# Eight early products of a folded weight placed between second products of a channel MLP, and one PSUM bank emptied by VectorE instead of ScalarE

## The chip, the cores and the metric

The kernel runs on one core of one Trainium2 chip. The metric is device time in microseconds of one execution, taken as the median of several executions. The engines are named as in the profile: PE is TensorE (matmul), PEld its weight load, DVE is VectorE, ACT is ScalarE, POOL is GpSimd, and SP is SyncE, which here only issues DMA.

## The reference, cut to what matters

```python
x = A_x                                   # (1, 2048, 640), float32
xn = layernorm(x)
return x + A(xn, wqkv, w_phi, wo) + B(xn, w1, b1, w2, b2)

# A: linear attention, 32 heads of 20
q, k, v = split_heads(xn @ wqkv)
pq, pk = q @ w_phi[h], k @ w_phi[h]       # per head
phi = lambda p: concat(softmax(p), softmax(-p))
o = phi(pq) @ (phi(pk).T @ v) / (phi(pq) @ phi(pk).sum(0) + 1e-6)
A = merge_heads(o) @ wo

# B: channel MLP with 1728 hidden units
B = gelu(layernorm(xn) @ w1 + b1) @ w2 + b2
```

All of it is float32. The kernel carries each float32 operand as two parts, a high one and a low one (`split`: ACT rounds the high part, DVE or POOL subtracts it to get the low part), and multiplies in three passes: high by high, high by low, low by high (`mm3`, L69 to L72).

## The kernel before, in words

The 2048 tokens are four blocks of 512 (b = 0 to 3), the 640 channels five chunks of 128 (KC = 5), the 1728 hidden units fourteen chunks of 128, taken in pairs (g = 0 to 6, j = 0 and 1).

**Order of the whole.** PE's order is written out by hand for the whole kernel (`manual_schedule` for PE, L513). From L562 to L865 the orders of DVE, ACT and POOL are written out too: each of them does its instructions in the order of the program text. From L865 to L1350 a list scheduler orders DVE, ACT and POOL by the program's order and by what it reckons to be ready, and after that they are by hand again. SP's queue of DMAs is put in order by the list scheduler throughout: a DMA whose buffer is free and whose data is there can be issued long before its place in the text. `tc.issue_after(loads[1])` keeps a DMA behind the load `loads[1]` in SP's queue, and nothing else.

**The channel MLP.** `passes(g, b, ws)` (L286) first does the pair's two first products (`first`, L275): for each j five chunks of three matmuls into one of the banks 0 to 2, then `gelu` (L282): ACT reads the bank, applies GELU with the bias into the tile `gt`, copies the high part to `hh`, and DVE subtracts for `hl`. After the first `yield` come the second products: for each output chunk m = 0 to 4, six matmuls (two j, three passes) into one of the banks 5 to 7 in turn, and a DVE instruction that adds the bank to `acc[b]` (L326 for g = 0, L328 otherwise). Three banks in turn mean that chunk m can only begin when the bank used three chunks earlier has been added up.

**Work beside it.** `tick()` is called after each three matmuls of a first product and after each j of a second one. It takes one step of the generator `mlp.beside`, and this is how other work is laced into the engines' orders.

**The start.** `p00` is the pair g = 0 on block 0, whose first products come from `half_first`; `p10` is the pair g = 1 on block 0. The order on PE is: `half_first`, the first products of `p10` (10 ticks), the second products of `p00` (10 ticks), the second products of `p10` (10 ticks), then `p01` and `p11` (block 1). The generator beside is `next_y` (L610), which makes the operand of block 1: at its fourth tick it sends the rows of mean and inverse deviation to DRAM on ACT's queue (L202) and loads them back, spread over 128 partitions, on SP's queue (`load_rows`, L207; this DMA is `loads[1]`). Later, once every two ticks, POOL subtracts the mean from a chunk of `acc[1]` (L635), DVE multiplies (L637), ACT copies the high part (L639), DVE subtracts (L641).

**The fold.** `wpt` is w_phi (120 rows, 6 groups of 6 by 20) with its first column subtracted from the 19 others (L662, one DVE instruction). The fold multiplies it into wk and wq: fourteen lists of up to four units (`units`), taken in seven jobs of two lists (`jobs`). For a job `raws` loads two tiles of transposed wk or wq (L683), `products` (L692) does four products of each tile into one of the banks 3 and 4 (`mlp.px`), and `split_w` (L700) moves each bank into the tiles `wk` by ACT (L711) and DVE (L713). The generator `prep` (L738) runs this beside `p11` and later passes; its first job's products are its first step. Tiles of the fold are in the pool `prep`, which is opened after the pool of the starting loads has been closed. In the same pool are `t` (rows of x for further statistics, L730) and `xq` (four tiles for chunks of blocks 2 and 3, loaded at L764, 10 loads in all, used far later).

**The start of the second part.** After the projections, whose exponentials are ACT's L934 (on POOL's L933), block 2 begins: L1094 makes `passes(0, 2, ws)`, and its two first products and the last key tile (`kv_tile`, L965) follow each other on PE, then the first products of block 3 (L1331). They share the banks 0 to 2 (`ptile`): j = 0 of block 2 has a first bank, j = 1 a second, the last key tile the third, and j = 0 of block 3 needs the first again. `issue_after(exps["q", 15].ins)` at L1095 keeps ACT's instructions of block 2 behind the last exponential on ACT.

Of the kernel before, what the change touches and what calls it, by code (L numbers as in the profile page):

```python
# [8 lines left out]
F32 = mybir.dt.float32  # L9
F32R = mybir.dt.float32r  # L10
AF = mybir.ActivationFunctionType
ALU = mybir.AluOpType
# [34 lines left out]
def f(ap):  # L47
    return ap.bitcast(F32)
# [3 lines left out]
def tile_kernel(ctx: ExitStack, tc: tile.TileContext, x, xT, wkT, wqT, wv, wphi, wo, w1, b1, w2, b2,  # L52
                ident, mmask, emask, vsel, out):
    nc = tc.nc
    ctx.enter_context(nc.allow_low_precision(reason="float32 operands are split exactly into float32r parts"))

    def split(hi, lo, src, scale=None, eng=nc.vector, first=nc.scalar):

        if scale is None:
            if first is nc.scalar:  # L60
                nc.scalar.activation(hi, src, AF.Copy)  # L61
            else:
                first.tensor_copy(hi, src)
            eng.tensor_tensor(lo, src, f(hi), op=ALU.subtract)  # L64
        else:
            nc.scalar.activation(hi, src, AF.Copy, scale=scale)
            nc.vector.scalar_tensor_tensor(lo, src, scale, f(hi), op0=ALU.mult, op1=ALU.subtract)

    def mm3(ps, lh, ll, rh, rl, first, last, **kw):  # L69
        nc.tensor.matmul(ps, lh, rh, start=first, stop=False, **kw)  # L70
        nc.tensor.matmul(ps, lh, rl, start=False, stop=False, **kw)  # L71
        nc.tensor.matmul(ps, ll, rh, start=False, stop=last, **kw)  # L72
# [47 lines left out]
    def mtile(i, dtype=F32):  # L120
        return mp.tile([P, 2, D if i < 5 else 512], dtype, name=f"m{i}")
# [82 lines left out]
    def load_rows(b, i=5):  # L204

        mr = mtile(i)
        loads[b] = nc.sync.dma_start(mr.rearrange("p a t -> p (a t)"),  # L207
                          (r_dram[1][0] if b == 1 else r_dram[2][b - 2]).rearrange("r t -> (r t)").unsqueeze(0).to_broadcast([P, 8 * P])).ins
        return mr

    loads = {}


    class Mlp:
# [60 lines left out]
        def first(self, g, j, b, w, gt, hh, hl):  # L275
            pz = self.ph()
            for kc in range(KC):
                mm3(pz, w[0][:, kc, :], w[1][:, kc, :], y[b][0][:, kc, :], y[b][1][:, kc, :], kc == 0, kc == KC - 1)
                self.tick()
            self.gelu(g, j, pz, gt, hh, hl)  # L280

        def gelu(self, g, j, pz, gt, hh, hl):  # L282
            nc.scalar.activation(gt, pz, AF.Gelu_apprx_tanh, bias=b1t[:, 2 * g + j:2 * g + j + 1])  # L283
            split(hh, hl, gt)

# [280 lines left out]
    def step(gen, n):  # L566
        for _ in range(n):
            next(gen, None)
# [38 lines left out]
    p00 = mlp.passes(0, 0, [wc[0], wc[1]], hid)  # L607
    next(p00)

    def next_y():  # L610
# [12 lines left out]
        for _ in range(8):  # L623
            yield

        for c in range(2, 4):
            parts[c][1]()
        for _ in range(5):
            yield
        xcs = {}  # L630
        for n in range(2 * KC + 5):
            c, i = divmod(n, 2)
            if i == 0 and c < KC:
                xcs[c] = xp.tile([P, D], F32, name="xb")[:, :512]
                nc.gpsimd.tensor_tensor(xcs[c], acc[1][:, c], mr[:, 0], op=ALU.subtract)  # L635
            if i == 0 and 0 <= (d := c - 1) < KC:
                nc.vector.tensor_tensor(xcs[d], xcs[d], mr[:, 1], op=ALU.mult)  # L637
# [12 lines left out]
    xs.close()  # L650
    with tc.issue_after(loads[1]):
# [2 lines left out]
    wkv = ExitStack()  # L654
    kvw = wkv.enter_context(tc.tile_pool(name="wkv", bufs=1, side="right", reuse_waits="tile"))
    wkv_ = [kvw.tile([P, KC, CN], F32R, name=f"wk{p}") for p in "hl"]
    rs = ExitStack()
    fp = rs.enter_context(tc.tile_pool(name="prep", bufs=2, side="right", reuse_waits="tile"))
    wpt = fp.tile([G6, 6, 6, DH], F32, name="wpt", bufs=1)
    with tc.issue_after(loads[1]):  # L660
        nc.sync.dma_start(wpt, wphi)
    nc.vector.tensor_tensor(wpt[:, :, :, 1:], wpt[:, :, :, 1:], wpt[:, :, :, 0:1].to_broadcast([G6, 6, 6, DF]), op=ALU.subtract)  # L662

    units = [(n, g, i) for n in "kq" for g in range(5) for i in range(KC)]
    units = [units[o:o + 4] for o in range(0, 50, 4)] + [[("kq", 5, i) for i in range(KC)]]

    def by_group(us):

        gs = [u[:2] for u in us]
        return [(*g, gs.index(g), gs.count(g), slice(us[gs.index(g)][2], us[gs.index(g)][2] + gs.count(g)))
                for g in dict.fromkeys(gs)]

    def raws(batch):
        ts = []
        for us in batch:
            raw = fp.tile([P, D], F32, name="raw")
            for n, g, u, nu, i in by_group(us):
                r, kk = g * G6, G6 if g < 5 else 2 * DH  # L680
                for j, one in enumerate(n):
                    with tc.issue_after(loads[1]):
                        nc.sync.dma_start(raw[j * kk:(j + 1) * kk, u * P:(u + nu) * P],  # L683
                                          {"k": wkT, "q": wqT}[one][r:r + kk, i.start * P:i.stop * P])
            ts.append(raw)
        return ts

    def prep_fold(batch, ts):

        parts = {"k": [(0, 0, DF)], "q": [(KQ, 0, B1F), (C3, B1F, DF)]}  # L690

        def products(us, raw):  # L692
            ps = mlp.px()
            for u, (n, g, i) in enumerate(us):
                nh = 6 if g < 5 else 4
                nc.tensor.matmul(ps[:, u * nh * DF:(u + 1) * nh * DF], raw[:nh * DH, u * P:(u + 1) * P], wpt[:nh * DH, g, :nh, 1:],  # L696
                                 start=True, stop=True)
            return us, ps
# [37 lines left out]
        yield from rows(2, 2, fp, mlp.px, 5)  # L736

    def prep():  # L738
        jobs = [units[o:o + 2] for o in range(0, 14, 2)]
# [14 lines left out]
        raw = fp.tile([P, D], F32, name="raw").rearrange("p (c d) -> p c d", c=KC)  # L754
# [5 lines left out]
        xs, hls, events = {}, {}, []  # L760

        def load(c, b):
            xs[c, b] = fp.tile([P, 512], F32, name="xq", bufs=4)
            nc.sync.dma_start(xs[c, b], xT[c * P:(c + 1) * P, b * 512:(b + 1) * 512])  # L764

        def centred(c, b):
            nc.gpsimd.tensor_tensor(xs[c, b], xs[c, b], mr[b][:, 0], op=ALU.subtract)
# [241 lines left out]
    for t, i in [(t, i) for t in range(14) for i in range(4)] + TAIL:  # L1009
        if (t, i) in ((4, 0), (8, 0)):  # L1010
            b = t // 4 + 1
# [3 lines left out]
        ps = proj(t, i)  # L1015
# [29 lines left out]
        if (t, i) == (11, 0):  # L1045
            mlp = Mlp((0, 3, 2, 1), ((1, 2), (0, 3)))
# [434 lines left out]
```

## Time and profile before

| what | value |
|---|---|
| median of 3 runs | 716.25 us (715.61 to 716.4) |
| the profiled execution | 716.96 us |
| its span, first to last instruction | 715.2 us |
| mean granted TensorE clock | 0.999 |
| busy: PE, DVE, POOL, ACT | 704.0, 513.1, 421.7, 342.1 us |
| fold products on PE (L696, 110 instructions) | 13.3 us |

A row of a timeline is: start in us from the first instruction, length in us, engine, line, operation, out<-in, shape, count, and in brackets the time for which the engine had been idle and what ended that. A row of the waits is: who waited for what, then total us, times, longest us. A row of the chain of waits is: start, us, what was on the chain. The engine names SPq and ACTq mean the queue of instructions that issue DMAs. A product of two plain float32 operands is two instructions on PE, so the eight products of a job are 16.

### The profile page before, as it was taken

To read this page: it belongs to the slowest core of one execution; us is meant where nothing else is said; L and a number is where in the kernel's file an instruction comes from. 1 tells how busy PE (TensorE), PEld (TensorE's weight loads), DVE (VectorE), ACT (ScalarE), POOL (GpSimd) and SP (SyncE) were. 2 spreads that over 40 slices of the span, in tenths; PEclk is the share of its full clock that TensorE was granted. 3 is DMA by queue.
4 is the path that set the end of the run, shared out by engine and by line. 5 is a ranking of instruction groups with operands and counts; after the bars stand their busy time and mean duration, and the time that the engine had idled before them with its cause. 6 is when DMAs were issued, how large, how long until landed. Compare 5 with 4: busy or idle time off the path is not lost.

```text
span 715.2 us, 9745 instructions
## 1 busy us (share of the span) xinstructions
PE 704.0 (98%) x3381; PEld 591.2 (83%) x3381; DVE 513.1 (72%) x820; ACT 342.1 (48%) x563; POOL 421.7 (59%) x360
## 2 busy tenths in 40 slices
PE   8989999999999999999999999999999999999998
PEld 6868888878878888888888888888888878888886
DVE  7776754978754788788888877747679785784632
ACT  6434453444433544554444547357666666560200
POOL 3521223657235998798787979548689887540400
PEclk9999999999999999999999999999999999999999
DMA  9813643474722226325500708864355568545222
GB/s 325 290 44 110 196 134 102 154 243 159 224 91 110 74 91 219 97 89 196 121 0 13 177 0 322 223 205 125 109 160 168 171 181 274 188 127 212 80 83 73
DMA packets 65767, 106.56 MB, mean 149 GB/s; under 512 B 7462, under 2 KB 31814, under 8 KB 63838
## 3 DMA queue, kind: packets, MB, share of 16 engines
q1 hardware_dynamic: 65414, 105.93, 46.5%
q8 instruction: 26, 0.43, 0.2%
q14 instruction: 23, 0.19, 0.1%
q10 hardware_dynamic: 304, 0.01, 0.0%
HBM read 71.37 MB, written 34.55 MB: 148 GB/s over the span
## 4 chain that ended last, share of the span: by engine, by line
PE 79%; DVE 7%; POOL 4%; DMA 4%; issue 3%; ACT 2%; SPq 1%; POOLq 0%; DVEq 0%; ACTq 0%
PE bank L898 23%; PE bank L70 16%; PE bank L72 15%; PE bank L71 15%; PE bank L968 2%; PE bank L696 2%; POOL m L933 2%; PE bank L1206 1%; PE bank L1207 1%; POOL w L64 1%; DMA t<-t 1%; DMA xq<-in_xT 1%; POOL m L944 1%; PE bank L323 1%; PE bank L324 1%
## 5 line engine op out<-in xcount | busy, mean ns | idle before, releaser
L898 PE MATMUL bank<-wkh,y 128*128 128x512 f32 (+1 forms) x480 | 139.5, 364 | 0.0
L70 PE MATMUL bank<-y,w 128*128 128x512 f32 (+1 forms) x294 | 114.4, 389 | 1.0 <-ACT m L283 1.0
L71 PE MATMUL bank<-y,w 128*128 128x512 f32 (+1 forms) x294 | 113.6, 387 | 0.0
L72 PE MATMUL bank<-y,w 128*128 128x512 f32 (+1 forms) x294 | 113.6, 386 | 0.0
L64 POOL TENSOR_TENSOR w<-r,w 128x640 fp32r<-128x640 f32 x32 | 52.2, 1645 | 98.8 <-ACT w L61 68.0
L70 PE MATMUL bank<-m,w 128*128 128x512 f32 x260 | 102.7, 395 | 3.5 <-DVE acc L328 3.2
L72 PE MATMUL bank<-m,w 128*128 128x512 f32 x260 | 101.3, 390 | 0.0
L71 PE MATMUL bank<-m,w 128*128 128x512 f32 x260 | 101.3, 389 | 0.0
L898 PEld LDWEIGHTS bank<-wkh,y 128*128 128x128 f32 x480 | 87.5, 188 | 13.3
L898 PE MATMUL bank<-wkl,y 128*128 128x512 f32 (+1 forms) x240 | 87.4, 364 | 0.0
L70 PEld LDWEIGHTS bank<-y,w 128*128 128x128 f32 x294 | 55.2, 188 | 12.8 <-ACT m L283 1.2
L72 PEld LDWEIGHTS bank<-y,w 128*128 128x128 f32 x294 | 55.2, 188 | 11.3
L71 PEld LDWEIGHTS bank<-y,w 128*128 128x128 f32 x294 | 55.2, 188 | 10.9
L934 ACT ACTIVATE m<-m,rs_all 128x1280 f32<-128x1280 f32 x32 | 43.7, 1365 | 42.9 <-POOL m L933 42.8
L70 PEld LDWEIGHTS bank<-m,w 128*128 128x128 f32 x260 | 48.8, 188 | 15.9 <-DVE acc L328 5.1
L936 DVE TENSOR_REDUCE sm<-m 128x64 f32<-128x1280 f32 x32 | 47.4, 1482 | 15.6 <-ACT m L934 15.4
L898 PE MATMUL bank<-w,y 128*128 128x512 f32 x240 | 57.4, 391 | 0.0
L72 PEld LDWEIGHTS bank<-m,w 128*128 128x128 f32 x260 | 48.8, 188 | 10.3
L71 PEld LDWEIGHTS bank<-m,w 128*128 128x128 f32 x260 | 48.8, 188 | 9.8 <-DVE m L458 0.2
L933 POOL TENSOR_TENSOR m<-m,mx 128x640 f32<-128x640 f32 (+2 forms) x48 | 44.4, 938 | 19.3 <-DVE mx L922 19.3
L328 DVE TENSOR_TENSOR acc<-bank,acc 128x512 f32<-128x512 f32 x70 | 46.9, 684 | 10.5 <-PE bank L72 5.4
L64 DVE TENSOR_TENSOR m<-m,m 128x512 fp32r<-128x512 f32 (+1 forms) x34 | 27.6, 819 | 35.5 <-ACT m L61 35.5
(182 smaller groups left out, 1461.6 us busy)
## 6 DMA issues: line engine op xcount, KB each, us to landing
r<-in_w SPq DMA_DIRECT2D x52, 320.0 KB
e<-e SPq DMA_DIRECT2D x40, 256.0 KB
e<-acc SPq DMA_DIRECT2D x52, 160.0 KB
acc<-in_xT SPq DMA_DIRECT2D x4, 1280.0 KB
t<-t SPq DMA_DIRECT2D x8, 512.0 KB
tf<-t SPq DMA_DIRECT2D x2, 1536.0 KB
xb<-in_x SPq DMA_DIRECT2D x8, 320.0 KB
xq<-in_xT SPq DMA_DIRECT2D x10, 256.0 KB
```

The lines of the kernel that those rows point to most:

```text
L64: eng.tensor_tensor(lo, src, f(hi), op=ALU.subtract)
L70: nc.tensor.matmul(ps, lh, rh, start=first, stop=False, **kw)
L71: nc.tensor.matmul(ps, lh, rl, start=False, stop=False, **kw)
L72: nc.tensor.matmul(ps, ll, rh, start=False, stop=last, **kw)
L323: nc.tensor.matmul(pw, w2h[:, ms], hh, start=False, stop=False)
L328: nc.vector.tensor_tensor(acc[b][:, m, :], pw, acc[b][:, m, :], op=ALU.add)
L696: nc.tensor.matmul(ps[:, u * nh * DF:(u + 1) * nh * DF], raw[:nh * DH, u * P:(u + 1) * P], wpt[:nh * DH, g, :nh, 1:], start=True, stop=True)
L898: nc.tensor.matmul(ps, lh[:, kc, c], rh[:, kc], start=n == 0, stop=n == 3 * KC - 1)
L933: subs[n, t] = nc.gpsimd.tensor_tensor(ep[:, s], a, b, op=ALU.subtract)
L934: exps[n, t] = nc.scalar.activation(e, e, AF.Exp, scale=rs_all[:, t:t + 1])
L936: nc.vector.tensor_reduce(sm, e.rearrange("p s (h f) -> p (s h) f", f=DH), axis=AX, op=ALU.add)
L968: nc.tensor.matmul(kvp[g // 2][:, (g % 2) * 240:(g % 2) * 240 + 240].rearrange("p (s f) -> p s f", s=4), v[:, g * VS:(g + 1) * VS], ft[:, ...
```

## The change

Two things are changed, and what hangs on them.

The first job of the fold comes earlier. Its pool is opened before the second products of `p00`, on the left side of the memory instead of the right. `wpt` is loaded there without `issue_after`. The two raw tiles of the first job are loaded in `next_y` right after `load_rows`. The subtraction in `wpt` stands in `next_y` at its eighth tick. The eight products themselves stand in the second products of `p10`, four after m = 2 and four after m = 3, and `prep` then starts with `split_w` of these. The loads of `xq` are put behind `loads[1]` in SP's queue.

The other: for g = 0, j = 0, b = 2 the bank of the first product is copied to `gt` by DVE, and GELU reads `gt`.

```diff
-            self.gelu(g, j, pz, gt, hh, hl)
-
-        def gelu(self, g, j, pz, gt, hh, hl):
+            self.gelu(g, j, pz, gt, hh, hl, (g, j, b) == (0, 0, 2))
+
+        def gelu(self, g, j, pz, gt, hh, hl, out=False):
+            if out:
+                nc.vector.tensor_copy(gt, pz)
+                pz = gt
             nc.scalar.activation(gt, pz, AF.Gelu_apprx_tanh, bias=b1t[:, 2 * g + j:2 * g + j + 1])
             split(hh, hl, gt)
...
     p00 = mlp.passes(0, 0, [wc[0], wc[1]], hid)
     next(p00)
 
+    rs = ExitStack()
+    fp = rs.enter_context(tc.tile_pool(name="prep", bufs=2, reuse_waits="tile"))
+    wpt = fp.tile([G6, 6, 6, DH], F32, name="wpt", bufs=1)
+    nc.sync.dma_start(wpt, wphi)
...
+    jobs = [units[o:o + 2] for o in range(0, 14, 2)]
+    first_raws, first_done = [], []
+
     def next_y():
...
         mr = load_rows(1)
+        first_raws.extend(raws(jobs[0]))
         for z in zs[2:]:
             z()
         for st in (s23, s47):
             step(st, 1)
-        for _ in range(8):
+        for _ in range(4):
+            yield
+        nc.vector.tensor_tensor(wpt[:, :, :, 1:], wpt[:, :, :, 1:], wpt[:, :, :, 0:1].to_broadcast([G6, 6, 6, DF]), op=ALU.subtract)
+        for _ in range(4):
             yield
...
     finish(p00)
-    finish(p10)
+    for m, _ in enumerate(p10):
+        if m in (2, 3):
+            first_done.append(products(jobs[0][m - 2], first_raws[m - 2]))
     finish(mlp.beside)
...
-    rs = ExitStack()
-    fp = rs.enter_context(tc.tile_pool(name="prep", bufs=2, side="right", reuse_waits="tile"))
-    wpt = fp.tile([G6, 6, 6, DH], F32, name="wpt", bufs=1)
-    with tc.issue_after(loads[1]):
-        nc.sync.dma_start(wpt, wphi)
-    nc.vector.tensor_tensor(wpt[:, :, :, 1:], wpt[:, :, :, 1:], wpt[:, :, :, 0:1].to_broadcast([G6, 6, 6, DF]), op=ALU.subtract)
...
-        done = [products(us, raw) for us, raw in zip(batch, ts)]
+        done = done or [products(us, raw) for us, raw in zip(batch, ts)]
         yield
...
-        ahead = raws(jobs[0])
+        ahead = []
         more = more_stats()
         for i, job in enumerate(jobs):
-            for k, _ in enumerate(prep_fold(job, ahead)):
+            for k, _ in enumerate(prep_fold(job, ahead, None if i else first_done)):
...
             xs[c, b] = fp.tile([P, 512], F32, name="xq", bufs=4)
-            nc.sync.dma_start(xs[c, b], xT[c * P:(c + 1) * P, b * 512:(b + 1) * 512])
+            with tc.issue_after(loads[1]):
+                nc.sync.dma_start(xs[c, b], xT[c * P:(c + 1) * P, b * 512:(b + 1) * 512])
```

`units`, `by_group`, `raws` and `products` are moved with their text unchanged.

More of the change, by code (lines that the diff above doesn't have):

```diff
@@ L608, in tile_kernel, with by_group, raws, products @@
     next(p00)
+    rs = ExitStack()
+    fp = rs.enter_context(tc.tile_pool(name="prep", bufs=2, reuse_waits="tile"))
+    wpt = fp.tile([G6, 6, 6, DH], F32, name="wpt", bufs=1)
+    nc.sync.dma_start(wpt, wphi)
+    units = [(n, g, i) for n in "kq" for g in range(5) for i in range(KC)]
+    units = [units[o:o + 4] for o in range(0, 50, 4)] + [[("kq", 5, i) for i in range(KC)]]
+    def by_group(us):
+        gs = [u[:2] for u in us]
+        return [(*g, gs.index(g), gs.count(g), slice(us[gs.index(g)][2], us[gs.index(g)][2] + gs.count(g)))
+                for g in dict.fromkeys(gs)]
+    def raws(batch):
+        ts = []
+        for us in batch:
+            raw = fp.tile([P, D], F32, name="raw")
+            for n, g, u, nu, i in by_group(us):
+                r, kk = g * G6, G6 if g < 5 else 2 * DH
+                for j, one in enumerate(n):
+                    with tc.issue_after(loads[1]) :
+                        nc.sync.dma_start(raw[j * kk:(j + 1) * kk, u * P:(u + nu) * P],
+                                          {"k": wkT, "q": wqT}[one][r:r + kk, i.start * P:i.stop * P])
+            ts.append(raw)
+        return ts
+    def products(us, raw):
+        ps = mlp.px()
+        for u, (n, g, i) in enumerate(us):
+            nh = 6 if g < 5 else 4
+            nc.tensor.matmul(ps[:, u * nh * DF:(u + 1) * nh * DF], raw[:nh * DH, u * P:(u + 1) * P], wpt[:nh * DH, g, :nh, 1:],
+                             start=True, stop=True)
+        return us, ps
+    jobs = [units[o:o + 2] for o in range(0, 14, 2)]
+    first_raws, first_done = [], []
     def next_y():
@@ L656, in tile_kernel, with prep_fold @@
     wkv_ = [kvw.tile([P, KC, CN], F32R, name=f"wk{p}") for p in "hl"]
-    rs = ExitStack()
-    fp = rs.enter_context(tc.tile_pool(name="prep", bufs=2, side="right", reuse_waits="tile"))
-    wpt = fp.tile([G6, 6, 6, DH], F32, name="wpt", bufs=1)
-    with tc.issue_after(loads[1]):
[L661 to L688, printed above, removed]
-        parts = {"k": [(0, 0, DF)], "q": [(KQ, 0, B1F), (C3, B1F, DF)]}
[L692 to L698, printed above, removed]
+    def prep_fold(batch, ts, done=None):
+        parts = {"k": [(0, 0, DF)], "q": [(KQ, 0, B1F), (C3, B1F, DF)]}
         def split_w(us, ps):
@@ L738, in prep @@
     def prep():
-        jobs = [units[o:o + 2] for o in range(0, 14, 2)]
-        ahead = raws(jobs[0])
+        ahead = []
         more = more_stats()
         for i, job in enumerate(jobs):
-            for k, _ in enumerate(prep_fold(job, ahead)):
+            for k, _ in enumerate(prep_fold(job, ahead, None if i else first_done)):
                 if k == 0 and i < 6:
```

## The prediction

> **What bounds the kernel now.** I read the busy times first, then PE's waits, then the timelines of PE, DVE and POOL around the waits that the change touches.
>
> ```profile
> PE 704.0 (98%) x3381; PEld 591.2 (83%) x3381; DVE 513.1 (72%) x820; ACT 342.1 (48%) x563; POOL 421.7 (59%) x360
> ```
>
> ```profile
> PE bank L70 <- DVE acc L328: 3.2, 4, 1.7
> ...
> PE bank L70 <- ACT m L283: 1.0, 1, 1.0
> ```
>
> PE is busy for 98% of the span and its order is fixed. Time is won only where PE stands still, or where work is taken out of a full stretch and put into a still one. The two waits are what the change can reach: four waits for an addition that frees a bank, and one for a GELU. Two of the four lie in the second products of `p10`:
>
> ```profile
> 37.83 0.40 PE L72 MATMUL bank<-m,w 128*128 128x512 f32 x1
> 39.89 0.51 PE L70 MATMUL bank<-m,w 128*128 128x512 f32 x1 [1.66 <-DVE acc L328]
> ...
> 41.15 0.39 PE L72 MATMUL bank<-m,w 128*128 128x512 f32 x1
> 42.17 0.50 PE L70 MATMUL bank<-m,w 128*128 128x512 f32 x1 [0.63 <-DVE acc L328]
> ...
> 51.15 1.94 PE L696 MATMUL bank<-wpt,raw 120*128 120x114 f32 x16
> 52.85 0.48 PE L70 MATMUL bank<-y,w 128*128 128x512 f32 x1
> 53.17 0.40 PE L71 MATMUL bank<-y,w 128*128 128x512 f32 x1
> 53.40 0.40 PE L72 MATMUL bank<-y,w 128*128 128x512 f32 x1
> ```
>
> The last matmul of m = 2 starts at 37.83 and m = 3 begins at 39.89; m = 3's last starts at 41.15 and m = 4 begins at 42.17. Where PE isn't held up, matmuls follow each other by 0.23 (53.17 to 53.40). The first job's 16 instructions stand in a full stretch, at 51.15. Who holds the banks back is seen on DVE and POOL:
>
> ```profile
> 27.79 0.69 DVE L64 TENSOR_TENSOR m<-m,m 128x512 fp32r<-128x512 f32 x1 [0.98 <-ACT m L61]
> 29.03 0.69 DVE L64 TENSOR_TENSOR m<-m,m 128x512 fp32r<-128x512 f32 x1 [0.55 <-ACT m L61]
> 29.64 2.10 DVE L326 SCALAR_TENSOR_TENSOR acc<-bank,b2t,acc 128x512 f32<-128x512 f32 x3
> 32.35 0.75 DVE L326 SCALAR_TENSOR_TENSOR acc<-bank,b2t,acc 128x512 f32<-128x512 f32 x1 [0.61 <-PE bank L72]
> 34.09 1.76 DVE L637 TENSOR_TENSOR xb<-xb,m 128x512 f32<-128x512 f32 x1 [0.98 <-POOL xb L635]
> ...
> 39.15 0.68 DVE L328 TENSOR_TENSOR acc<-bank,acc 128x512 f32<-128x512 f32 x1
> ...
> 42.03 0.68 DVE L637 TENSOR_TENSOR xb<-xb,m 128x512 f32<-128x512 f32 x1
> ...
> 46.84 0.85 DVE L662 TENSOR_TENSOR wpt<-wpt 120x684 f32<-120x684 f32 x1
> ```
>
> ```profile
> 29.71 3.10 POOL L64 TENSOR_TENSOR w<-r,w 128x640 fp32r<-128x640 f32 x2 [4.41 <-ACT w L61]
> 32.75 7.61 POOL L635 TENSOR_TENSOR xb<-acc,m 128x512 f32<-128x512 f32 x5
> ```
>
> From 34.09 on DVE has no idle time and lags behind PE; it can't start sooner, since its first L637 waits for POOL's L635, which stands behind two L64 on POOL. The addition at 39.15 ends at 39.83, and PE starts at 39.89. So these stalls are set by the chain ACT, POOL, DVE; products put into them don't lengthen it.
>
> **Part 1, the products.** Taken out: without them L71 would start 0.23 after 51.15 and starts at 53.17, so 1.79 us leave a full stretch. Put in: eight instructions take half of 52.85 - 51.15, that is 0.85. The first eight start at 38.06 (37.83 + 0.23) and end at 38.91; the bank comes at 39.83, so they cost nothing (cover 0.9 us; without it 0.85). The second eight run from 41.38 to 42.23, against a start of 42.17 before: +0.06, with a switch taken as +0.1.
>
> Their inputs: the subtraction (0.85) leaves its place at 46.84, where PE waits for nothing (the waits above have only L328 and L283), and goes between the L64 of 27.79 and that of 29.03, since the eighth tick falls between the two first products. Two L64 or additions in a row start 0.60 apart at 0.68 length, so it starts at 28.39, and the next L64 at 29.16 instead of 29.03. The idle 0.61 at 32.35 and 0.98 at 34.09 swallow 0.13. What is queued behind it on DVE are that L64 and the additions of `p00`; they move by 0.14, while the fourth of them still waits 0.61 for PE at 32.35, so PE isn't waiting for them. But the L64 now ends at 29.86, and POOL starts its own at 29.71. The two hinder each other: L637 takes 1.76 while POOL runs and 0.68 at 42.03, when POOL is done. If POOL waits for DVE, its chain and the stalls end 0.15 later. I take +0.15, with bounds -1.1 (the interleaving of DVE with POOL comes out shorter; no more, since the stalls are 2.9 with their restarts, of which 1.7 is filled) and +0.69 (a whole L64).
>
> The SBUF — State Buffer page of the Trainium skill, section "Who interferes with whom", speaks against the change here: a DVE instruction with two SBUF inputs and a POOL instruction that reads SBUF exclude each other for a whole instruction, and the one that starts first has it. By it the sum holds while DVE starts first; if POOL came first it would be the third rival below. The 1.76 and 0.68 agree with it.
>
> The DMAs that move:
>
> ```profile
> 13.45 3.89 SPq L764 DMA_DIRECT2D xq<-in_xT  x4
> ...
> 28.40 0.48 SPq L661 DMA_DIRECT2D wpt<-in_wphi  x1
> ```
>
> ```profile
> 27.54 4.23 DMA m<-r
> ```
>
> ```profile
> 32.00:38.00 6.00, 5.83 (x26) 4.36 (x24) 4.67 (x5) 1.06 (x2) 6.00 (x5) 1.00 0.98 294
> ```
>
> SP is free at 13.45: it issues four `xq` loads (1 MB) there although they stand far later in the text. In the changed kernel these wait for `loads[1]`, and `wpt` (0.34 MB), which doesn't, takes their place: issued 15 us ahead of 28.39, where `m<-r`, a larger one, takes 4.23 to land. The three raw loads follow `m<-r` at 27.54 at once, before 38.06 even if they were the last of that burst, which fills the DMA engines until about 37.5. With less in front of it `m<-r` may come sooner; that gains nothing, as POOL's L64 occupy POOL until 32.75. The `xq` loads move to about 33 to 37, still far ahead of use. The moved pool changes which old tiles the next stage's tiles lie on; the fold's last reader is POOL itself just ahead of that stage's clearing, so 0.
>
> Part 1: -1.79 + 0.10 + 0.15 = **-1.54**.
>
> **Part 2, the bank.**
>
> ```profile
> 435.25 0.24 PE L972 MATMUL bank<-w,v 128*128 128x160 f32 x1
> ...
> 435.60 0.40 PE L71 MATMUL bank<-y,w 128*128 128x512 f32 x1
> ...
> 438.60 0.39 PE L72 MATMUL bank<-y,w 128*128 128x512 f32 x1
> ...
> 443.36 0.24 PE L972 MATMUL bank<-w,v 128*128 128x160 f32 x1
> ...
> 444.96 0.39 PE L71 MATMUL bank<-y,w 128*128 128x512 f32 x1
> ```
>
> ```profile
> 441.20 1.37 ACT L934 ACTIVATE m<-m,rs_all 128x1280 f32<-128x1280 f32 x1 [4.28 <-POOL m L933]
> ...
> 443.88 0.69 ACT L283 ACTIVATE m<-bank,b1t 128x512 f32<-128x512 f32 x1
> ```
>
> ```profile
> 437.67 2.01 DVE L64 TENSOR_TENSOR w<-m,w 128x1280 fp32r<-128x1280 f32 x1
> 442.60 1.49 DVE L936 TENSOR_REDUCE sm<-m 128x64 f32<-128x1280 f32 x1 [2.92 <-ACT m L934]
> ...
> 446.38 1.15 DVE L1107 COPY t<-bank 127x480 f32<-127x480 f32 x2
> ...
> 449.29 0.65 DVE L64 TENSOR_TENSOR m<-m,m 128x512 fp32r<-128x512 f32 x1
> ```
>
> Block 2's j = 0 is done on PE at 439.0 (438.60 + 0.39), but ACT's GELU stands behind an exponential that waits for POOL, and the load of a table (441.20 + 1.37 to 443.88): its bank is free at 444.57, and PE waits. The same switch, L972 to L71, takes 0.35 without a wait (435.25 to 435.60) and 1.60 here: the stall is worth 1.25. The added copy costs about 0.6 (1.15 for two of 480 columns; bounds 0.57 and the 0.69 of an addition) in DVE's idle 2.92 us: from 439.68 it ends near 440.3, three us ahead of PE's need at 443.4. What is queued behind it is L936, which waits for ACT until 442.60 anyway. ACT's GELU stays where it is and then feeds j = 0's parts as before. Late next would be the second products of block 2, at 451.56 now:
>
> ```profile
> 451.56 0.39 PE L70 MATMUL bank<-m,w 128*128 128x512 f32 x1
> ```
>
> They would begin near 450.3; the low part of j = 1 is ready at 449.94 (449.29 + 0.65) and needed three matmuls later still. The gain stands: **-1.25**.
>
> **Sum.** -1.54 - 1.25 = -2.79. The profiled execution took 716.96, of which 715.2 is the span; the span becomes 712.4 and that execution 714.2. The runs' median is 716.25, 0.71 below that execution; less 2.79 it is **713.5**.
>
> **The rivals.**
>
> First, the copy doesn't come ahead of L936: DVE's order there is made by a list scheduler. Behind L936 the copy would start at 444.0, end later than the GELU that it replaces, and part 2 would bring nothing: 714.7. For it: L936 is earlier in the text. Against it: PE's products end 3.6 us before L936 can start.
>
> Second, part 1 is given back at the next wait of this kind:
>
> ```profile
> 145.45 0.06 DVE acc L328
> ...
> 148.66 5.54 DMA xq<-in_xT
> ...
> 197.28 0.50 PE bank L70
> ```
>
> This chain runs through `xq` loads, POOL and DVE and ends in a stall at 197.28. If a load in it were tied to SP's queue instead of PE's ticks, PE would come early and wait the 1.54 there: 715.0. Against it: the chain is entered from an addition of PE's own bank at 145.45, so it moves along.
>
> Third, POOL's L64 starts before DVE's, by the mechanism above: DVE's L64 then waits until 31.26 (half of 3.10 from 29.71), it and the four additions behind it (0.6 + 4 x 0.68) end near 34.6, and L637 starts 0.5 late; in place of 0.15 that gives 713.8. It decides if DVE's L64 starts after 29.71, 0.55 later than reckoned.
>
> Fourth, slower: `wpt` lands late. DVE stands in order at the subtraction and everything behind it slips. With four additions and the L64 behind it (0.85 + 0.6 + 4 x 0.68 = 4.2, against 34.09) this is free until 29.9; each us later costs one. It eats the whole gain at 32.7. If SP issued `wpt` behind `m<-r`, as at 28.40, it would land between 31.8 (when `m<-r` has landed) and 37.5 (when the burst ends); the middle, 34.6, costs 4.7 and gives 718.1. Against it: SP is free at 13.45 and nothing holds `wpt` back.
>
> Fifth, it does nothing: 716.3, if both orders came out other than written. PE's order is by hand, which speaks against it.
>
> **How the numbers follow.** Forecast 0.59, first 0.10, second 0.08, third 0.10, fourth 0.08, fifth 0.05. The forecast's own range is 712.4 (bound -1.1) to 714.1 (bound +0.69). To leave out no more than 2 in 10 with something for what I don't see, the range runs to the fifth case: 712.4 to 716.3. A measurement here tells about 0.2%, 1.4 us, from no change. Faster: the forecast and the third almost whole, 0.67, and part of the first and second, 0.08: 0.75. Slower: the fourth and a little of the fifth, 0.10. Within: 0.15.
>
> **What would show it.** Right: L696 twice before 42.3 with eight instructions each, m = 3 still beginning near 39.9 and m = 4 near 42.3; no L696 at 51; the subtraction near 28.4 without a wait for a DMA; a copy on DVE near 439 (less the shift) and no wait of L70 for ACT's L283. Wrong: an idle time of DVE ahead of the subtraction, m = 3 beginning after 40.5, longer waits at 157 or 197, or the copy behind L936.

## The result, and the profile after

| | before | after |
|---|---|---|
| median | 716.25 us (715.61 to 716.78, 7 runs) | 713.46 us (712.59 to 715.25, 7 runs) |
| ratio after to before, 95% interval | | 0.9964 (0.9952 to 0.9976) |
| the profiled execution | 716.96 us | 713.46 us |
| its span | 715.2 us | 711.6 us |

The medians differ by 2.79 us, the sum that was forecast; the interval makes it 1.7 to 3.4. The two profiled spans differ by 3.6. Which part of this is the change's is read below from where PE's times move. The lines of the changed file are numbered 3 higher near the bank's additions, 5 higher near L667, 45 higher near L637 and 8 higher beyond L764; the products' L696 is now L644.

The busy times of the changed kernel:

```profile
PE 703.8 (99%) x3381; PEld 592.2 (83%) x3381; DVE 514.0 (72%) x821; ACT 342.0 (48%) x563; POOL 421.4 (59%) x360
```

PE does the same work, 3381 instructions and 704 us; DVE has one more, the copy. So the gain is idle time of PE. The waits of PE in the changed kernel, of which the two that bear on the change are shown:

```profile
PE bank L71 <- DVE m L461: 0.9, 1, 0.9
PE bank L70 <- DVE acc L331: 0.8, 1, 0.8
```

Of the four waits for an addition (3.2 us in all) one of 0.8 is left, the wait for ACT's GELU is gone, and there is a new one, of L71 for DVE's L461, that the prediction doesn't have. PE's timeline of the changed kernel around the second products of `p10`, the first products of `p01`, the last key tile and the second products of block 2:

```profile
37.77 0.39 PE L72 MATMUL bank<-m,w 128*128 128x512 f32 x1
37.99 1.04 PE L644 MATMUL bank<-wpt,raw 120*128 120x114 f32 x8
39.83 0.50 PE L70 MATMUL bank<-m,w 128*128 128x512 f32 x1 [0.79 <-DVE acc L331]
...
41.32 1.04 PE L644 MATMUL bank<-wpt,raw 120*128 120x114 f32 x8
42.13 0.48 PE L70 MATMUL bank<-m,w 128*128 128x512 f32 x1
...
43.60 0.40 PE L70 MATMUL bank<-y,w 128*128 128x512 f32 x1
...
51.33 0.39 PE L71 MATMUL bank<-y,w 128*128 128x512 f32 x1
...
439.87 0.24 PE L980 MATMUL bank<-w,v 128*128 128x160 f32 x1
...
440.22 0.40 PE L71 MATMUL bank<-y,w 128*128 128x512 f32 x1
...
446.84 0.39 PE L70 MATMUL bank<-m,w 128*128 128x512 f32 x1
...
551.75 0.50 PE L71 MATMUL bank<-m,w 128*128 128x512 f32 x1 [0.95 <-DVE m L461]
```

Each half of the products lies in what was a stall: the first leaves 0.79 of the 1.66, the second takes all of the 0.63, and m = 3 and m = 4 begin where they did (39.89 and 42.17 before). At the end of the first products, where the sixteen instructions stood, L71 comes at 51.33 instead of 53.17. The switch from the key tile to L71 takes 0.35 (439.87 to 440.22), as it did where nothing held it; with the wait it took 1.60.

One more view of the kernel before is needed, PE's timeline at two waits for an addition that the changed kernel's profile doesn't have:

```profile
156.82 0.50 PE L70 MATMUL bank<-m,w 128*128 128x512 f32 x1 [0.54 <-DVE acc L328]
...
197.28 0.50 PE L70 MATMUL bank<-m,w 128*128 128x512 f32 x1 [0.36 <-DVE acc L328]
```

With it the difference between the two profiles is laid out along the span, each row the start of the same matmul after less before:

| at (after) | shift so far | what came to it |
|---|---|---|
| 37.8 and 43.6 | -0.06 | there from the start |
| 51.33 | -1.84 | -1.78: part 1 |
| about 155 | -2.73 | -0.89: the wait of 0.54 and its restart are absent |
| about 195 | -3.48 | -0.75: the wait of 0.36 and its restart are absent |
| 440.22 | -4.74 | -1.26: part 2 |
| 551.75 | -3.61 | +1.13: the new wait of 0.95 and its restart |
| the last matmul | -3.52 | +0.09, spread out |

Part 1 and part 2 make -3.04. The other three rows, -0.51 in all, have nothing to do with either part on the face of it, and experiments 3, 4 and 11 are about them.

What DVE did in the changed kernel (timeline), at the subtraction (L667) and at the copy (L284):

```profile
28.32 0.86 DVE L667 TENSOR_TENSOR wpt<-wpt 120x684 f32<-120x684 f32 x1
29.10 0.68 DVE L64 TENSOR_TENSOR m<-m,m 128x512 fp32r<-128x512 f32 x1
...
34.03 1.75 DVE L682 TENSOR_TENSOR xb<-xb,m 128x512 f32<-128x512 f32 x1 [0.97 <-POOL xb L680]
...
39.09 0.68 DVE L331 TENSOR_TENSOR acc<-bank,acc 128x512 f32<-128x512 f32 x1
...
436.09 0.68 DVE L284 COPY m<-bank 128x512 f32<-128x512 f32 x1
439.09 1.49 DVE L944 TENSOR_REDUCE sm<-m 128x64 f32<-128x1280 f32 x1 [2.32 <-ACT m L942]
```

The subtraction starts at 28.32 with no idle time ahead of it, so `wpt` was there. The copy ends at 436.77, 3.2 us ahead of PE's need. POOL, in the changed kernel:

```profile
29.63 3.12 POOL L64 TENSOR_TENSOR w<-r,w 128x640 fp32r<-128x640 f32 x2 [4.41 <-ACT w L61]
32.70 7.60 POOL L680 TENSOR_TENSOR xb<-acc,m 128x512 f32<-128x512 f32 x5
```

POOL's pair of L64 overlaps the end of DVE's (29.78) by 0.15, and yet L680 follows 3.07 after its start; before the change, with an overlap of 0.01, it was 3.04. POOL was held by 0.03 at most.

### The profile page after: what moved, and what is told of

It is laid out like the page before. It is cut to its first block, busy times and chain, and to the rows that moved or that the text cites. A ratio compares the mean times of both kernels' runs of the same rounds, so it can differ in the third digit from the quotient of the medians.

```text
span 711.6 us, 9745 instructions
## 1 busy us (share of the span) xinstructions
PE 703.8 (99%) x3381; PEld 592.2 (83%) x3381; DVE 514.0 (72%) x821; ACT 342.0 (48%) x563; POOL 421.4 (59%) x360
## 5 line engine op out<-in xcount | busy, mean ns | idle before, releaser
L71 PE MATMUL bank<-y,w 128*128 128x512 f32 (+1 forms) x294 | 113.7, 387 | 0.0
L64 POOL TENSOR_TENSOR w<-r,w 128x640 fp32r<-128x640 f32 x32 | 52.2, 1645 | 96.0 <-ACT w L61 67.0
L71 PE MATMUL bank<-m,w 128*128 128x512 f32 x260 | 101.3, 390 | 0.9 <-DVE m L461 0.9
L71 PEld LDWEIGHTS bank<-y,w 128*128 128x128 f32 x294 | 55.2, 188 | 10.9
L944 DVE TENSOR_REDUCE sm<-m 128x64 f32<-128x1280 f32 x32 | 47.4, 1481 | 15.0 <-ACT m L942 14.8
L71 PEld LDWEIGHTS bank<-m,w 128*128 128x128 f32 x260 | 48.8, 188 | 11.1 <-DVE m L461 1.4
L906 PEld LDWEIGHTS bank<-w,y 128*128 128x128 f32 x240 | 44.4, 188 | 8.5
```

The costliest lines, as they stand in the source:

```text
L906: nc.tensor.matmul(ps, lh[:, kc, c], rh[:, kc], start=n == 0, stop=n == 3 * KC - 1)
L944: nc.vector.tensor_reduce(sm, e.rearrange("p s (h f) -> p (s h) f", f=DH), axis=AX, op=ALU.add)
```

## The experiments

The theory: the two parts act apart and add up; part 1 is worth what its sixteen instructions take out of a full stretch, since the stalls are set by the chain ACT, POOL, DVE; part 2 is worth the stall behind the GELU. The rivals: a part is given back at a later wait, the place of the products matters more than their leaving, the subtraction or the loads cost something that a cover hides. Diffs are against the changed kernel, unless said otherwise, and lines are numbered by each kernel's own file.

### 1 and 2: each part alone

Experiment 1 is part 1 alone:

```diff
-            self.gelu(g, j, pz, gt, hh, hl, (g, j, b) == (0, 0, 2))
+            self.gelu(g, j, pz, gt, hh, hl)
```

> Part 1 alone (GELU reads the bank again). My theory: 1.54 us faster than before, about 714.7 (ratio 0.9979); PE's wait for ACT's L283 near 441 is back with about 1.0 us, and the order near 38 to 53 is as in the changed kernel. The rival that part 1 is given back later: no gain, 716.3, with longer waits near 155 or 195. In the profile of the changed kernel the waits near 157 and 197 are gone (1.2 us with their restarts): if the moved loads did that, they are gone here too; if it is chance from one execution to the next, they may be there or not.

714.14 us against 716.63 for the kernel before, ratio 0.9969 (0.9957 to 0.998), that is -2.2 us (-3.1 to -1.4). PE's timeline of it:

```profile
440.00 0.24 PE L980 MATMUL bank<-w,v 128*128 128x160 f32 x1
441.23 0.50 PE L70 MATMUL bank<-y,w 128*128 128x512 f32 x1 [0.99 <-ACT m L286]
441.57 0.40 PE L71 MATMUL bank<-y,w 128*128 128x512 f32 x1
```

The wait for ACT is back in its old size, and L980 to L71 takes 1.57.

Experiment 2 is the kernel before with the copy alone:

```diff
-            self.gelu(g, j, pz, gt, hh, hl)
+            self.gelu(g, j, pz, gt, hh, hl, (g, j, b) == (0, 0, 2))
```

> Part 2 alone (the products stay where they were, only the copy on VectorE is added). My theory: 1.25 us faster than before, about 715.0 (ratio 0.9983); PE's L70 after the last key tile starts 0.08 after L972 instead of 1.26. Rival, that the copy only moves the wait: 716.3, with a new wait of PE within the next 20 us. If the sum of both parts is what the change is worth, this and part 1 alone add up to 2.8 us; the waits near 157 and 197 should be as in the kernel before if the moved loads of part 1 removed them.

715.51 us, ratio 0.9983 (0.9974 to 0.9992), -1.2 us (-1.9 to -0.6). PE's timeline of it:

```profile
442.54 0.24 PE L975 MATMUL bank<-w,v 128*128 128x160 f32 x1
...
442.88 0.40 PE L71 MATMUL bank<-y,w 128*128 128x512 f32 x1
```

0.34 from L975 to L71, against 1.57 in experiment 1 and 1.60 before. Neither part needs the other: -2.2 and -1.2 stand against -2.6 to -4.4 for both together (experiment 3, against the same runs of the kernel before).

### 3, 4 and 11: the two kernels once more

Experiment 3 is the changed kernel unchanged. Experiments 4 and 11 are the kernel before, with one execution each.

> The changed kernel a second time, to see which waits of PE come and go. My theory: 713.5 (ratio 0.9961). The wait of 0.95 near 552 for DVE's L461 stands where DVE's L461 and POOL's L1265 started within 0.01 us of each other; if that is a race for who comes first, it will be absent in some profiles and the time 1.1 us shorter in these executions; if it comes from the changed kernel's order, it is there again with the same length.

> The kernel before a second time, one profile. If the waits near 157 (0.54) and 197 (0.36) depend on how long loads take in an execution, at least one of them has another length here, by 0.2 us or more; if they belong to the kernel's order, both are there as in the first profile, within 0.1. The waits at 39.9 (1.66), 42.2 (0.63) and 444.6 (1.02) should be there in either case.

> The kernel before a third time, one profile, for the waits near 157 and 197. They were 0.54 and 0.36, then none. If they are chance, any mix of lengths from 0 to about 0.7; if the second profile was the exception, 0.5 and 0.4 again. The waits at 39.9, 42.2 and 444.6 stay within 0.05 of 1.66, 0.63 and 1.0.

Experiment 3 took 712.81 us, ratio 0.9952 (0.9939 to 0.9964). Its profile has a span of 710.8 and no wait of L71 near 552. Experiment 4 took 715.54 with a span of 713.8 and no wait near 157 or 197; experiment 11 took 716.42 with a span of 714.6 and a wait of 0.47 near 157. So both kernels have waits that come and go from one execution to the next. The spans of experiments 3 and 4, which have none of them, differ by 3.0, the sum of the two parts' rows above. And the two rows are the same in every profile: with the products in their old place (before, experiments 2, 4 and 11) the stretch from 45.2 to 52.0 of the changed kernel takes 1.81 to 1.82 longer, and with GELU reading the bank (before, experiments 1, 4 and 11) the one from 205 to 440.2, which holds the switch, takes 1.21 to 1.25 longer.

How the wait near 552 is decided is seen by setting DVE's and POOL's timelines side by side. In the first profile of the changed kernel:

```profile
549.86 1.83 DVE L461 TENSOR_TENSOR m<-m,m 128x512 fp32r<-128x512 f32 x1
```

```profile
549.87 1.28 POOL L1265 TENSOR_TENSOR acc<-acc,rx 128x512 f32<-128x512 f32 x1
```

And in experiment 3, the same kernel:

```profile
550.20 0.68 DVE L461 TENSOR_TENSOR m<-m,m 128x512 fp32r<-128x512 f32 x1
```

```profile
550.22 1.81 POOL L1265 TENSOR_TENSOR acc<-acc,rx 128x512 f32<-128x512 f32 x1
```

One of the two takes its short time while the other takes 0.5 (POOL) or 1.15 (DVE) more. When it is DVE, its m is late and PE waits 0.95. Experiment 9 has it the first way again (DVE 1.84, POOL 1.29, a wait of 0.93); the other eleven profiles, those of the kernel before among them, have it the second way. The traces give the starts in nanoseconds. DVE's record leads POOL's by 11 to 36 ns in the eleven profiles in which DVE has its short time; it leads by 2 ns in the first profile of the changed kernel and trails by 5 ns in experiment 9. So the order of arrival goes with the outcome, and here it turns on a few nanoseconds. The Trainium skill, SBUF — State Buffer, section "Who interferes with whom", says that a DVE instruction with two SBUF inputs and a POOL instruction that reads SBUF exclude each other, and that the order of issue decides who is held. The runs agree, but for the lead of 2 ns, with which DVE was held all the same.

Whether part 1 makes the waits near 157 and 197 rarer isn't settled. Against the first profile of the changed kernel, the stretch from 150 to 205, which holds both with the slower matmuls that restart behind them, is longer by 1.60, 0.10, 1.16 and 0.65 us in the four profiles without part 1 (before, experiments 4, 11 and 2), and by 0, 0.05, 0.05, 1.03, 0.89, 0.06, 1.11, -0.05 and 0.95 in the nine with it (the first one, experiments 3, 1 and 5 to 10). Experiments 7 and 8 have one more such wait, of 0.56 and 0.43, near 472 and 475. What decides these waits stays open.

### 5 and 6: other places for the products

Experiment 5 puts them after m = 0 and 1, in front of the stalls; experiment 6 after m = 3 and 4, so that the second four lie beyond them.

```diff
-        if m in (2, 3):
-            first_done.append(products(jobs[0][m - 2], first_raws[m - 2]))
+        if m in (0, 1):
+            first_done.append(products(jobs[0][m], first_raws[m]))
```

```diff
-        if m in (2, 3):
-            first_done.append(products(jobs[0][m - 2], first_raws[m - 2]))
+        if m in (3, 4):
+            first_done.append(products(jobs[0][m - 3], first_raws[m - 3]))
```

> The changed kernel with the eight products after m = 0 and m = 1 of p10 instead of m = 2 and m = 3, thus ahead of the stalls and not in them. My theory, that DVE's row of work sets when m = 3 and m = 4 begin: m = 2 begins about 1.4 later, but m = 3 again near 39.8 and m = 4 near 42.05 without waiting for products; same time as the changed kernel, 713.4 (ratio to before 0.996). The rival, that products are free only inside the stalls: 0.85 to 1.7 us slower than the changed kernel, 714.3 to 715.2.

> The changed kernel with the products after m = 3 and m = 4, so that the second four stand behind the last stall. My theory: the first four fill the wait of m = 4, m = 3 waits its whole 1.66 again, and the second four cost 0.85 less the slack that block 1's operand leaves (DVE ends it near 46.3, PE needs it near 46.6): 0.5 to 0.85 us slower than the changed kernel, 714.0 to 714.4, with p01 beginning near 44.4 instead of 43.6. Rival, that the operand of block 1 holds PE up there in any case and hides the second four too: no difference, 713.5, with a wait of PE in p01's first product.

Experiment 5: 713.87 us against 716.32, ratio 0.9969 (0.9958 to 0.998). PE's timeline of it:

```profile
39.81 0.51 PE L70 MATMUL bank<-m,w 128*128 128x512 f32 x1 [0.31 <-DVE acc L331]
...
42.10 0.51 PE L70 MATMUL bank<-m,w 128*128 128x512 f32 x1 [0.62 <-DVE acc L331]
43.58 0.39 PE L70 MATMUL bank<-y,w 128*128 128x512 f32 x1
```

m = 3, m = 4 and `p01` begin within 0.03 of the changed kernel. All the products came before the first wait and took 1.35 us from it: what counts is that they lie ahead of a bank that DVE will free at 39.8 and 42.1 whatever PE does. This is the direct evidence that DVE's work, and not PE's, sets these starts.

Experiment 6: 714.53 us, ratio 0.9983 (0.9973 to 0.9992), 0.66 above experiment 5, which was measured beside it. PE's timeline:

```profile
39.90 0.50 PE L70 MATMUL bank<-m,w 128*128 128x512 f32 x1 [1.67 <-DVE acc L331]
...
43.67 1.04 PE L644 MATMUL bank<-wpt,raw 120*128 120x114 f32 x8
44.48 0.48 PE L70 MATMUL bank<-y,w 128*128 128x512 f32 x1
```

The stall ahead of m = 3 has its old 1.67, and the four products behind m = 4 move `p01` to 44.48, 0.88 later than in the changed kernel. Half the products outside a stall cost what half of them cost before, 0.85 by the prediction's row.

### 7: the subtraction in a full stretch of DVE

```diff
-        nc.vector.tensor_tensor(wpt[:, :, :, 1:], ..., op=ALU.subtract)
         for _ in range(4):
             yield
...
+            if n == 4:
+                nc.vector.tensor_tensor(wpt[:, :, :, 1:], ..., op=ALU.subtract)
```

> The changed kernel with the subtraction in wpt taken out of DVE's idle stretch near 28 and put between DVE's L682 and L686 near 37.5, where DVE has no idle time. My theory: m = 3 begins 0.8 later (40.6), all behind it too, 714.3; since POOL works at that time the subtraction may be held up or hold POOL up, up to 1.7. Rival, that POOL's L680 and not DVE sets the stalls: m = 3 stays near 39.8 and the time at 713.5.

715.28 us, ratio 0.9986 (0.9976 to 0.9996), 1.4 above experiment 5. DVE's timeline of it:

```profile
37.62 1.95 DVE L685 TENSOR_TENSOR wpt<-wpt 120x684 f32<-120x684 f32 x1
...
41.16 0.68 DVE L331 TENSOR_TENSOR acc<-bank,acc 128x512 f32<-128x512 f32 x1
```

PE's timeline of it:

```profile
39.62 1.15 PE L644 MATMUL bank<-wpt,raw 120*128 120x114 f32 x8 [1.23 <-DVE wpt L685]
41.90 0.50 PE L70 MATMUL bank<-m,w 128*128 128x512 f32 x1 [1.13 <-DVE acc L331]
```

Beside POOL's five subtractions the same instruction takes 1.95 instead of 0.86. The addition for m = 3 comes at 41.16 instead of 39.09, and m = 3 at 41.90 instead of 39.83: 2.07 later, above the 0.8 to 1.7 expected, which reckoned too little for POOL's work beside it. The cover that the prediction named for the subtraction (DVE's idle time at 32 and 34, ahead of POOL's first chunk) is worth that much in the profile, and the 2.07 are still there at 200. The profiles' spans differ by 2.1 from experiment 5 (713.6 against 711.5), the medians by the 1.4 above; the two intervals allow either.

### 8: `wpt` behind the rows

The load of `wpt` goes behind the load of the rows in SP's queue, the fourth rival's case:

```diff
-    nc.sync.dma_start(wpt, wphi)
...
         mr = load_rows(1)
+        with tc.issue_after(loads[1]):
+            nc.sync.dma_start(wpt, wphi)
```

> The changed kernel with the load of wpt behind loads[1] in SP's queue, as in the kernel before: the fourth rival of the prediction. By its reckoning wpt lands between 30.8 and 36.6, DVE stands at the subtraction until then, it is free until 29.9 and each us later costs one: 714.4 to 720.2, in the middle 717.3. If DVE's later work had slack that the reckoning missed, the time stays near 713.5 although DVE waits for a DMA ahead of the subtraction.

718.15 us, ratio 1.0025 (1.0014 to 1.0037): slower than before, and 4.4 above the changed kernel by the two ratios. DVE's timeline of it:

```profile
31.34 0.87 DVE L668 TENSOR_TENSOR wpt<-wpt 120x684 f32<-120x684 f32 x1 [2.69 <-DMA wpt<-in_wphi]
32.12 2.02 DVE L64 TENSOR_TENSOR m<-m,m 128x512 fp32r<-128x512 f32 x1
...
37.83 0.75 DVE L329 SCALAR_TENSOR_TENSOR acc<-bank,b2t,acc 128x512 f32<-128x512 f32 x1 [1.70 <-PE bank L72]
38.49 1.05 DVE L683 TENSOR_TENSOR xb<-xb,m 128x512 f32<-128x512 f32 x1
```

PE's timeline:

```profile
34.86 0.79 PE L70 MATMUL bank<-m,w 128*128 128x512 f32 x1 [3.75 <-DVE acc L329]
35.45 0.63 PE L71 MATMUL bank<-m,w 128*128 128x512 f32 x1
...
37.16 0.63 PE L72 MATMUL bank<-m,w 128*128 128x512 f32 x1
...
44.04 0.47 PE L70 MATMUL bank<-m,w 128*128 128x512 f32 x1
```

And the stretch behind the wait (window, length; busy time of PE, PEld, DVE, ACT, POOL; granted clock; DMA share; GB/s):

```profile
34.00:38.50 4.50, 3.64 (x10) 2.88 (x11) 2.80 (x6) 0.00 (x0) 4.50 (x4) 0.62 0.95 358
```

The subtraction starts at 31.34, 1.44 beyond the 29.9 to which the prediction called it free, and by "each us later costs one" that is 1.44. DVE's first L683 is 4.46 later than in the changed kernel (38.49 against 34.03) and m = 3 is 4.21 later. Three things came on top of the 1.44. DVE's L64 now stands behind POOL's and takes 2.02 instead of 0.68: 1.34. PE stood still for 3.75 us, and then its granted clock is 0.62 in this stretch and matmuls follow each other by 0.43 instead of 0.23, so the six of the bank that DVE's fourth addition needs take 2.93 (34.86 to 37.79) instead of the 1.65 of the six of m = 3 in the changed kernel, which also stand behind a wait (39.83 to 41.48): 1.28. The rest, 0.4, is what the sum leaves over; it is put down to that addition's wait for PE even at full clock, since PE had been held by DVE, and no run shows it by itself. The Trainium skill, TensorE: Matmul & The Clock Gate, section "What's actually happening", gives an idle window of about 3.4 us after which the clock is halved; the wait of 3.75 here agrees, and waits of 1.67 in other runs show nothing of it.

### 9: the loads of `xq` early again

```diff
-            with tc.issue_after(loads[1]):
-                nc.sync.dma_start(xs[c, b], xT[...])
+            nc.sync.dma_start(xs[c, b], xT[...])
```

> The changed kernel with the loads of xq free again (not behind loads[1]), so that they can go out near 14 behind wpt. My theory: m<-r is issued up to 1 us later than in the changed kernel (27.5 instead of 26.6), which POOL's two L64 cover; no difference to the changed kernel, 713.5. Rival, that the rows' load sets POOL's first L680: stalls near 40 end up to 1 us later, 714.4.

714.49 us against 716.45, ratio 0.9972 (0.996 to 0.9984); its profile has the chance wait near 552. SP's queue in it:

```profile
15.04 4.32 SPq L772 DMA_DIRECT2D xq<-in_xT  x4
28.86 0.33 SPq L207 DMA_DIRECT2D m<-r  x1
```

In the changed kernel SP issues the rows' load at 26.58. With 1 MB of `xq` behind `wpt` it is 2.28 later. It waits for the store of the rows, 4 KB on ACT's queue, whose issue in experiment 9 is

```profile
23.05 0.53 ACTq L202 DMA_DIRECT2D r<-sr  x1
```

against 23.02 in the changed kernel's profile. The store isn't issued later, and by the trace it is the store's landing that releases the load. From the store's issue to the load's it takes 2.2 us with neither `wpt` nor the `xq` loads in front (experiment 8), 2.9 to 4.3 with `wpt` alone (seven profiles), 4.1 to 4.4 with the `xq` loads alone (before, experiments 2, 4 and 11) and 5.8 here, with both. POOL, in experiment 9:

```profile
33.10 7.59 POOL L680 TENSOR_TENSOR xb<-acc,m 128x512 f32<-128x512 f32 x5 [0.34 <-issue]
```

POOL's first chunk starts at 33.10 instead of 32.70, and POOL is idle for 0.34 ahead of it. The profile names no releaser, but the rows' load, issued at 28.86, would land at 33.09 by the 4.23 that it took in the kernel before. m = 3 comes at 40.22 instead of 39.83. So the load is later by more than the 1 us expected, POOL's L64 cover most of the 2.28, and 0.4 gets through, in part as the rival had it. By this profile the move of the loads is worth 0.4 once `wpt` stands in front of them. By the ratios experiment 9 is 0.6 and 1.4 us above the changed kernel's two measurements, with waits that come and go in both, so the times alone don't give a price.

### 10: the additions of `p10` late

A step further: the additions for m = 2 to 4 of `p10` wait until `next_y` is done, and DVE's L686 stands two ticks later, so that DVE comes to the additions that free banks (m = 0 and 1) ahead of it.

```diff
+                if held is not None and m > 1:
+                    held.append(lambda m=m, pw=pw: nc.vector.tensor_tensor(acc[b][:, m, :], pw, acc[b][:, m, :], op=ALU.add))
...
-    p10 = mlp.passes(1, 0, [wc[2], wc[3]])
+    held = []
+    p10 = mlp.passes(1, 0, [wc[2], wc[3]], held=held)
...
-        for n in range(2 * KC + 5):
+        for n in range(2 * KC + 6):
...
-            if i == 0 and 0 <= (d := c - 2) < KC:
+            if i == 0 and 0 <= (d := c - 3) < KC:
...
+    for add in held:
+        add()
```

> A further step: in p10 DVE adds m = 0 and m = 1 ahead of the subtractions for block 1's low parts (each of these two ticks later), and the additions of m = 2 to 4 come behind all of them. My theory, that DVE's order and not its load sets m = 3: the addition of m = 0 ends near 38.0 instead of 39.8, m = 3 begins near 38.9 right behind the first four products, m = 4 near 41.2, p01 near 42.6; 0.9 us faster than the changed kernel, 712.5 (ratio to before 0.9948). Rival, that the operand of block 1 then comes too late: a wait of PE in p01's first product and no gain, 713.5.

712.98 us, ratio 0.9955 (0.9942 to 0.9969). PE's timeline of it:

```profile
38.86 0.47 PE L70 MATMUL bank<-m,w 128*128 128x512 f32 x1
...
43.06 0.39 PE L70 MATMUL bank<-y,w 128*128 128x512 f32 x1
```

m = 3 begins at 38.86, right behind the first four products, as expected (38.9): DVE's order sets it. `p01` starts at 43.06, 0.54 earlier than in the changed kernel and 0.46 later than the 42.6 expected. In this profile the 0.54 don't last: the waits between 150 and 205 (0.22 near 154, with its restart, and what follows) take 0.95 more than in the changed kernel's first profile. By time it isn't told apart from the changed kernel, whose two medians are 713.46 and 712.81. That the step brings anything is not shown.

## Why the prediction was right, and where not

**The stalls belong to the chain ACT, POOL, DVE.** Right. m = 3 and m = 4 begin where they did, and experiment 5 puts all the products ahead of them without moving either. DVE's end of the chain is shown by experiments 7 and 10, which move m = 3 by DVE's work alone, POOL's by experiment 9 (0.40 later on POOL, 0.39 on PE); ACT's rests on one row, the wait of POOL's L64 for it, and no run changes it.

**Taken out, 1.79.** Right: 1.78 in the first pair of profiles, 1.81 to 1.82 over all of them.

**The second four, +0.10.** Too much: m = 4 begins 0.04 earlier than before, +0.02 against the 0.06 by which that whole stretch lies earlier.

**POOL held by DVE's moved L64, +0.15.** This is the step that failed. The overlap of 0.15 came about as reckoned (29.78 against 29.63), but POOL's L680 came 3.07 after its L64 instead of 3.04. Part 1 is -1.78 and not -1.54. The step took the whole overlap of two records for time in which one holds the other. The rows near 550 speak against that, by an estimate: in experiment 3 POOL's L1265 takes 1.81 beside DVE, and 1.28 where it isn't held, so it gets going 0.53 after its start, at 550.75, while DVE's record ends at 550.88; with DVE held, in the first profile, it gets going at 551.01 (549.86 + 1.83 - 0.68) and POOL's record ends at 551.15. The last 0.13 to 0.14 of a record hold nobody there, and of an overlap of 0.15 that leaves 0.02. The bounds of this term hold a slip as well: -1.1 and +0.69 stand for the term itself and so replace its +0.15, which gives 712.2 to 714.0 and not 712.4 to 714.1; the 713.46 lies in either.

**The subtraction costs nothing.** Right (28.32 forecast as 28.39, no idle time ahead of it). Its cover is worth 2.07 us in the profile of experiment 7; its bare length of 0.85 would have been the wrong price for it.

**`wpt` is early; the moved loads and pool cost nothing.** Right: issued at 13.48, ahead of everything. What the prediction didn't see is that with `wpt` there the `xq` loads have to go: left at 15, they cost 0.4 in the profile of experiment 9. Behind the rows' load they went out at 29.75 to 32.66, and not at 33 to 37.

**The copy, -1.25.** Right to 0.01 in the first pair (-1.26), and to 0.04 over all profiles (1.21 to 1.25; 1.57 against 0.34 in experiments 1 and 2). The copy took 0.68, the upper of its two bounds, and it didn't matter.

**Late next: none in block 2.** Right: the second products begin 4.72 earlier (451.56 to 446.84), the switch ahead of them 4.74.

**The sum.** The parts make -3.04 and not -2.79, and experiments 3 and 4 show 3.0. That the first medians differ by 2.79 to the hundredth is chance: waits of up to about 1 us come and go in both kernels, and the intervals of the two measurements, -3.4 to -1.7 and -4.4 to -2.6 us, hold either.

**The rivals.** The copy came ahead of L944, 3.0 before it, not behind. Nothing was given back near 157 or 197 in the two profiles of the changed kernel and in that of part 1 alone. POOL's L64 didn't start first; its mechanism was seen in experiment 8, where DVE's L64 took 2.02. The fourth rival is real where SP's order is the other (experiment 8, 718.15 against the 718.1 worked out), but its price was right for a wrong reason: `wpt` came 3.3 us earlier than the middle taken (the subtraction at 31.34, not 34.6), and each us of lateness beyond 29.9 cost 2.9 and not one.

## What to carry to other kernels

Here a stall that another engine set was filled for nothing by independent work that lay ahead of it in PE's order and was shorter than the stall, and the gain was the time that this work had taken where it stood, within 0.03 us; work put behind the last stall gained nothing. Price a cover by what runs beside it, not by the length of the covered instruction: an instruction of 0.86 us cost 2.07 beside POOL, and a load 1.44 us too late became 4.2. Before a difference between two profiles is explained, lay out the shift along the span and profile both kernels again: here half a microsecond net of 3.5 belonged to waits that come and go.

## What was not expected of the hardware

A few nanoseconds in the start order of DVE and POOL go with which of two instructions takes 1.15 us (DVE) or 0.5 (POOL) longer, and so with whether PE waits 0.95: with DVE 11 to 36 ns ahead POOL is held, with 2 ns ahead or 5 behind DVE is; the same kernel shows both. The last 0.13 us or so of a record of either engine held the other no longer, by the estimate above. One wait of 3.75 us of PE cost the addition behind it about 1.3 us more, in six matmuls 0.43 apart instead of 0.23. And with 1 MB of loads from 15 on in SP's queue, besides the 0.34 MB of `wpt`, a 4 KB store issued at 23.05 on ACT's queue landed so much later that the load of the rows, which waits for it, went out at 28.86 and not at 26.58.
